# Earlier loads around attention backward: wqkv and pk/va chunks transposed into freed buffers, x over grad_out, dv without its denominator column

## The chip, the cores and the metric

The kernel runs on one core of one Trainium2 chip. The metric is the device time of one execution in microseconds. All executions quoted here were of the undisturbed (fast) kind. A run of an experiment is always timed in rounds with the kernel before on the same chip. A **ratio** is the mean time of one kernel's fast runs over that of the other's fast runs of the same rounds, so it is not quite the ratio of the medians that stand beside it.

## The reference

One transformer block, forward and backward, for x of 2048 rows and 640 columns in bf16: layer norm, linear attention with 32 heads of 20, layer norm, gated MLP of width 1728. Outputs are the block's result and the gradients of x, wqkv, wo, w1, w3, w2.

```python
phi = lambda t: jnp.where(t > 0, t + 1, jnp.exp(t)) + 1e-6
pq, pk = phi(q), phi(k)
kv = einsum("bhsd,bhse->bhde", pk, v);  z = einsum("bhsd->bhd", pk)
o  = einsum(pq, kv) / (einsum(pq, z)[..., None] + 1e-6)
h  = x + reshape(o) @ wo          # of layernorm(x)
h2 = h + (silu(n @ w1) * (n @ w3)) @ w2     # n = layernorm(h)
# then jax.vjp with grad_out
```

## The kernel before

The kernel keeps z as a 21st column of each head's kv block, so a head has DA = 21 columns where the gradient of v has DH = 20. It was tuned already: TensorE runs nearly without a gap, and all else is arranged beside it. The stretch that matters here has five stages, named after their matmuls:

1. **ghn loop** (attention backward), one step for each of 16 row tiles t: 54 matmuls for the gradient at the second norm from gg (loaded as `ggb`, 1.7 MB for two tiles), and between them `h<-woT,ghT` and three more small products of earlier tiles. SyncE loads and transposes what they need.
2. **gwo**: 160 matmuls for the gradient of wo, with the last tiles of attention backward between them.
3. **two jobs and trk**: two blocks of the gradient of wqkv (16 matmuls each, a "job"), and 12 transposes of the kv gradient.
4. **dv loop**: 16 steps that make the gradients of v (L910) and k (L731 into g_k), from pk and va loaded transposed in four chunks, with jobs between.
5. **jobs and gxn**: more jobs, then the product with wqkv transposed (`wqT`) from the transposed gradients (`gT`).

```python
    def b_gT(t):                                   # in the ghn loop, one step after b_ghn(t)
        ghT[t] = br.tile([P, DT, P], BF16, name="ghT", bufs=2)
        dmaT(out=ghT[t][:], in_=g_h[:, t, :])
    # ... (cut)
    def load_kT(c):
        pkT[c] = dx.tile([P, DT, W], BF16, name="pkT", bufs=2)
        dmaT(out=pkT[c][:], in_=pk_d[c * W:(c + 1) * W, :])
        vaT[c] = dx.tile([P, CT, W], BF16, name="vaT", bufs=2)
        dmaT(out=vaT[c][:], in_=va_d[c * W:(c + 1) * W, :])
    # ... (cut)
    for t in range(ST):                            # the dv loop
        c, i = divmod(t, TPC)
        acc = [d_acc(), d_acc()]                   # two of six PSUM banks
        for m, a, b, bank, off, first in ND:
            T.matmul(acc[bank][:, off:off + (b - a) * DA], lhsT=pkT[c][:, m, i * P:(i + 1) * P],
                     rhs=gkv_b[:, m, a * DA:b * DA], ...)
        # ... (ScalarE evicts 20 of 21 columns to g_v: cut)
        if t in (3, 4, 5, 6, 8, 9, 10, 12):
            next(jobs, None)
        gphi(vaT[c][:, :, i * P:(i + 1) * P], gkvT, pkb[c][:, i, :], g_k[:, t, :], d_acc)
        if i == 3 and c + 2 < SC:
            load_pk(c + 2)                         # plain pk rows, for VectorE
            load_kT(c + 2)
        if t == 7:
            wqT = U1.tile([P, 15, D], BF16, name="wqT", tag="D")
            dmaT(out=wqT[:], in_=A_wqkv[:, :])     # the transposed load of wqkv
```

`dma` and `dmaT` are issued by SyncE in program order; a store of a finished block is issued by ScalarE.

Of the kernel before, what the change touches and what calls it, by code (L numbers as in the profile page):

```python
# [8 lines left out]
P = 128  # L9
BF16 = mybir.dt.bfloat16  # L10
F32 = mybir.dt.float32
# [6 lines left out]
S, D, H, F = 2048, 640, 32, 1728  # L18
DH = D // H
DA = DH + 1  # L20
C, CP = H * DA, 768
ST, DT, CT = S // P, D // P, CP // P
FT, FP = 14, 1792
FL = F - 13 * P
W, SC, TPC = 512, 4, 4
HD = D // 2
NG = 27
# [35 lines left out]
def kernel(  # L63
# [19 lines left out]
    V, A, T, G, SY = nc.vector, nc.scalar, nc.tensor, nc.gpsimd, nc.sync  # L83
    dma, dmaT = SY.dma_start, SY.dma_start_transpose
# [4 lines left out]
    xS = rows(A_x.flatten_outer_dims())  # L89
# [4 lines left out]
    out2S, out3S, out4S, out5S = rows(out_2), rows(out_3), rows(out_4), rows(out_5)  # L94
# [4 lines left out]
    pk_d = dram.tile([S, D], BF16, name="pk_d")  # L99
    va_d = dram.tile([S, CP], BF16, name="va_d")  # L100
# [6 lines left out]
    def pool(name, side="left", space=None):  # L107
        kw = dict(space=space) if space is not None else dict(side=side)
        return tc.alloc_tile_pool(name=name, bufs=1, reuse_waits="tile", **kw)

    cp = pool("cp")
    U1 = pool("u1")
# [34 lines left out]
    ln1, ln2 = Stats("ln1"), Stats("ln2")  # L147
# [4 lines left out]
    ps = pool("p1p", space=PSUM)  # L152
# [143 lines left out]
    for t in range(ST):  # L296
        g, i = divmod(t, TPC)
# [8 lines left out]
        if i == 0 and g > 0:  # L306
# [3 lines left out]
               in_=v[:, :, 0:HD].rearrange("p j (h e) -> p j h e", e=DH))  # L310
# [4 lines left out]
        if i == TPC - 1:  # L315
            sl = slice(g * TPC, (g + 1) * TPC)
# [10 lines left out]
    ps = pool("pap", space=PSUM)  # L327
# [180 lines left out]
    for c in range(SC):  # L508
# [8 lines left out]
        for fc in range(FT):  # L517
# [9 lines left out]
            if c == SC - 1 and fc == 0:  # L527
                g2 = U1.tile([P, ST, D], BF16, name="g2", tag="Q")
# [18 lines left out]
    pf.release()  # L547
    ps.release()

    br = pool("br", "right")  # L550
    ps = pool("pcp", space=PSUM)
    load_hh(1)
# [24 lines left out]
    ggb = {}  # L577

    def load_gg(j):
        ggb[j] = br.tile([P, NG, 2 * P], BF16, name="ggb", bufs=2)  # L580
        dma(out=ggb[j][:], in_=gg_d[:, j * 2 * P:(j + 1) * 2 * P].rearrange("(c p) w -> p c w", p=P))

    for fc in range(FT):
        b, i = divmod(fc, 4)
        n = P if fc < FT - 1 else FL
        acc = ps.tile([P, 2, 512], F32, name="gw", bufs=4)
        for j in range(2):
            for t in range(ST):
                T.matmul(acc[:n, j, 0:HD], lhsT=hb[b][:, t, i * P:i * P + n], rhs=g2[:, t, j * HD:(j + 1) * HD],  # L589
                         start=(t == 0), stop=(t == ST - 1))  # L590
        ob = br.tile([P, D], BF16, name="gw2o", bufs=2)
# [19 lines left out]
    g_h = bl.tile([P, ST, D], BF16, name="g_h")  # L611
    g_q = bl.tile([P, ST, D], BF16, name="g_q")
    bo = pool("bo")
    o_sb = bo.tile([P, ST, D], BF16, name="o_sb")
    ps = pool("pbp", space=PSUM)
# [111 lines left out]
    def gphi(lhsT, rhs, src, out, alloc):  # L727

        acc = [alloc(), alloc()]
        for cc, a, b, bank, off, first in GP:  # L730
            T.matmul(acc[bank][:, off:off + (b - a) * DH], lhsT=lhsT[:, cc, :], rhs=rhs[:, cc, a * DH:b * DH],  # L731
                     start=first, stop=True, skip_group_check=True)
        for bank, (a, b) in enumerate(((0, SPLIT_C), (SPLIT_C, H))):
            cs = slice(a * DH, b * DH)
            V.scalar_tensor_tensor(out=out[:, cs], in0=src[:, cs], scalar=1.0, in1=acc[bank][:, 0:(b - a) * DH],
                                   op0=ALU.min, op1=ALU.mult)
# [1 line left out]
    def b_gpq(t):  # L738
        gphi(gndT[t], kvbdT, pqb[t], g_q[:, t, :], h1)

    def wo_job(m):
        acc = ps.tile([P, 2, 512], F32, name="gwo", tag="ghn", bufs=2)
        for t0, j in ((0, 0), (0, 1), (8, 0), (8, 1)):
            for t in range(t0, t0 + 8):
                T.matmul(acc[:, j, 0:HD], lhsT=o_sb[:, t, m * P:(m + 1) * P], rhs=g_h[:, t, j * HD:(j + 1) * HD],  # L745
                         start=(t == 0), stop=(t == ST - 1))
            yield
        ob = br.tile([P, D], BF16, name="gw2o", bufs=2)
        A.copy(out=ob[:].rearrange("p (j n) -> p j n", j=2), in_=acc[:, :, 0:HD])
        A.dma_start(out=out3S[:, m, :], in_=ob[:])  # L750

    def wo_jobs():
        for m in range(DT):
            yield from wo_job(m)

    b_load(0)
    b_load(1)
    wog = wo_jobs()
    for t in range(ST):
        g = b_ghn(t)  # L760

        def part():
            next(g, None)
# [24 lines left out]
        if u >= 0:  # L788
            b_gndT(u)


    xnN = {}
    b_load_q(ST - 1)

    def load_x():
        xnN[0] = U1.tile([P, ST, D], BF16, name="xnN", tag="Q")
        for i in range(SC):
            dma(out=xnN[0][:, i * TPC:(i + 1) * TPC, :], in_=xS[:, i * TPC:(i + 1) * TPC, :])

    def norm_x(a, b):  # L800
        for j in range(a, b):
            ln1.norm(xnN[0][:, j, :], xnN[0][:, j, :], j)

    def part(n=1):
        for _ in range(n):
# [2 lines left out]
    a, b, c = ST - 1, ST - 2, ST - 3  # L808
    part()
    ln_rest.pop(a)()  # L810
    load_x()
    b_gT(b)
    part()
    b_gkv(c)
    part()
    b_go(b)
    part(2)
    b_gpq(c)
    part(3)
    b_gT(a)  # L820
    part()
    b_go(a)
    b_gndT(b)
    b_gkv(b)
    part(2)
    b_gpq(b)
    norm_x(0, 8)
    part(2)
    b_gndT(a)
    b_gkv(a)  # L830
    gkv_b = kvbd
    for m, (e0, e1) in enumerate(M_H):
        bank, off = KV_SLOT[m]
        V.tensor_tensor(out=gkv_b[:, m, e0 * DA:e1 * DA], in0=gkv[:, bank, off:off + M_W[m]],
                        in1=mask[:, m, 0:M_W[m]], op=ALU.mult)
    part(2)
    b_gpq(a)
    norm_x(8, ST)
    xnN = xnN[0]
    part(20)  # L840
    br.release()


    dx = pool("dx", "right")
    pkT, vaT, pkb, gb = {}, {}, {}, {}

    def load_kT(c):
        pkT[c] = dx.tile([P, DT, W], BF16, name="pkT", bufs=2)
        dmaT(out=pkT[c][:], in_=pk_d[c * W:(c + 1) * W, :])
        vaT[c] = dx.tile([P, CT, W], BF16, name="vaT", bufs=2)  # L850
        dmaT(out=vaT[c][:], in_=va_d[c * W:(c + 1) * W, :])

    def load_pk(c):
        pkb[c] = dx.tile([P, TPC, D], BF16, name="pkb", bufs=2)
        dma(out=pkb[c][:], in_=pk_v[:, c * TPC:(c + 1) * TPC, :])

    obs = U1.tile([P, 8, 320], BF16, name="obs", tag="W6")
    cnt = [0]
    njob = 2

    def grad_job(lhs, m, rhs, n, out):

        acc = ps.tile([P, 512], F32, name="job", bufs=njob)
        for t in range(ST):
            T.matmul(acc[:, 0:n], lhsT=lhs[:, t, m * P:(m + 1) * P], rhs=rhs(t), start=(t == 0),  # L865
                     stop=(t == ST - 1))
        ob = obs[:, cnt[0] % 8, 0:n]
        cnt[0] += 1
        A.copy(out=ob, in_=acc[:, 0:n])  # L869
        A.dma_start(out=out, in_=ob)  # L870
# [4 lines left out]
    def wq_jobs(ks):  # L875
        for m in range(DT):
            for k in ks:
                for j in range(2):
                    grad_job(xnN, m, half(gqkv[k], j), HD, out2S[:, m, k * D + j * HD:k * D + (j + 1) * HD])
                    yield  # L880

    for c in range(2):
        load_pk(c)
        load_kT(c)
    ps.release()
    ps = pool("pdp", space=PSUM)
    bo.release()
    bv = pool("bv")
    g_v = bv.tile([P, ST, D], BF16, name="g_v")
    hnN = bv.tile([P, ST, D], BF16, name="hnN")  # L890
    g_k = U1.tile([P, ST, D], BF16, name="g_k", tag="S0")
    gqkv = [g_q, g_k, g_v]
    jobs = wq_jobs((0,))
    next(jobs)
    gkvT = dx.tile([P, CT, D], BF16, name="gkvT")
    for cc, dcs in BLOCKS:
        tr = ps.tile([P, len(dcs), P], BF16, name="trk", tag="job", bufs=njob)
        for i, dc in enumerate(dcs):
            T.transpose(tr[:, i, :], gkv_b[:, dc, cc * P:(cc + 1) * P], ident[:])
        V.tensor_copy(out=gkvT[:, cc, dcs[0] * P:(dcs[-1] + 1) * P].rearrange("p (i q) -> p i q", q=P), in_=tr[:])  # L900
    next(jobs)

    def d_acc():
        return ps.tile([P, 512], F32, name="dkv", bufs=6)

    for t in range(ST):
        c, i = divmod(t, TPC)
        acc = [d_acc(), d_acc()]
        for m, a, b, bank, off, first in ND:
            T.matmul(acc[bank][:, off:off + (b - a) * DA], lhsT=pkT[c][:, m, i * P:(i + 1) * P],  # L910
                     rhs=gkv_b[:, m, a * DA:b * DA], start=first, stop=True, skip_group_check=True)
        for bank, (a, b) in enumerate(((0, SPLIT_D), (SPLIT_D, H))):
            o_ = g_v[:, t, a * DH:b * DH].rearrange("p (h d) -> p h d", d=DH)
            i_ = acc[bank][:, 0:(b - a) * DA].rearrange("p (h e) -> p h e", e=DA)[:, :, 0:DH]
            A.copy(out=o_, in_=i_)
        if t in (3, 4, 5, 6, 8, 9, 10, 12):
            next(jobs, None)
        gphi(vaT[c][:, :, i * P:(i + 1) * P], gkvT, pkb[c][:, i, :], g_k[:, t, :], d_acc)
        if i == 3 and c + 2 < SC:
            load_pk(c + 2)  # L920
            load_kT(c + 2)
        if t == 7:
            wqT = U1.tile([P, 15, D], BF16, name="wqT", tag="D")
            dmaT(out=wqT[:], in_=A_wqkv[:, :])  # L924
    for _ in jobs:
        pass
    dx.release()


    ex = pool("ex", "right")  # L930
# [30 lines left out]
    ps = pool("pep", space=PSUM)  # L961
    njob = 2
# [22 lines left out]
    ps = pool("pfp", space=PSUM)  # L985
    njob = 8
# [40 lines left out]
```

## Time and profile before

| | kernel before |
|---|---|
| median, first four runs | 874.43 us (873.98 to 874.99) |
| span of the profiled execution | 873.8 us |
| TensorE busy | 851.7 us (97%) |

Columns of a timeline are start and length in us, engine, source line, operation, output and inputs, shape and count.

### The profile page before, as it was taken

The numbers are of one execution on the slowest core, as the hardware profiler recorded it, in microseconds if no ns is written. First come the engines' busy times: TensorE is split into PE (matmuls) and PEld (weight loads), VectorE is DVE, ScalarE is ACT, GpSimd is POOL, SyncE is SP. The second block draws the span as 40 slices with busy tenths as digits, with TensorE's granted clock in tenths as the row PEclk, the third lists the DMA queues.
The fourth block names the chain that finished last, engine by engine and source line by source line (L and its number), as shares of the span: only waits on it lengthen the run. The fifth ranks groups of instructions, "written<-read, shape, count | busy, mean of one in ns | idle before, by whom it ended". The sixth has DMA issues, their size and how long they took to land.

```text
span 873.8 us, 16002 instructions
## 1 busy us (share of the span) xinstructions
PE 851.7 (97%) x6263; PEld 582.2 (67%) x6263; DVE 441.0 (50%) x1134; ACT 334.6 (38%) x643; POOL 20.4 (2%) x42
## 2 busy tenths in 40 slices
PE   6999999999999999999999999999989999999998
PEld 4776555555555555777767777777757777777776
DVE  7777688888888777200146566555312434300000
ACT  4556877655655666011111111123422333322221
POOL 3100000000000000000000000000000000000000
PEclk9999999999999999999999999999989999999999
DMA  9978583364365652999477789459996588477671
GB/s 283 251 236 272 157 253 124 110 166 146 110 162 141 198 175 99 233 242 275 138 178 170 179 202 202 90 183 187 227 199 200 119 174 172 110 172 166 157 147 38
DMA packets 338027, 153.81 MB, mean 176 GB/s; under 512 B 238112, under 2 KB 336672, under 8 KB 337952
## 3 DMA queue, kind: packets, MB, share of 16 engines
q1 hardware_dynamic: 319440, 139.60, 64.9%
q10 hardware_dynamic: 18512, 13.20, 5.1%
q8 instruction: 49, 0.80, 0.4%
q14 instruction: 26, 0.21, 0.1%
HBM read 45.20 MB, written 50.02 MB: 109 GB/s over the span
## 4 chain that ended last, share of the span: by engine, by line
PE 82%; DMA 4%; SPq 2%; DVE 1%; ACT 1%; issue 0%; ACTq 0%; DVEq 0%
PE mm L413 20%; PE job L865 20%; PE ghn L643 12%; PE gxn L954 7%; PE gw L589 7%; PE o L466 7%; DMA ghT<-g_h 2%; PE h L700 2%; PE gwo L745 2%; PE at L371 2%; SPq L924 1%; DMA vaT<-va_d 1%; DMA oT<-o_t 1%; PE h L731 1%; PE nd L334 1%; SPq L948 0%
## 5 line engine op out<-in xcount | busy, mean ns | idle before, releaser
L413 PE MATMUL mm<-hnT,w 128*128 128x512 bf16 x540 | 128.1, 379 | 0.9 <-ACT hnT L408 0.9
L865 PE MATMUL job<-gb,hnN 128*128 128x288 bf16 x960 | 117.8, 286 | 0.0
L865 PEld LDWEIGHTS <-hnN 128*128 128x128 bf16 x960 | 93.9, 98 | 23.7
L643 PEld LDWEIGHTS <-ggb 128*128 128x128 bf16 x864 | 83.0, 98 | 31.1 <-issue 0.3
L413 PEld LDWEIGHTS <-w 128*128 128x128 bf16 x540 | 52.3, 98 | 61.4 <-issue 1.4
L869 ACT CAST obs<-job 128x288 bf16<-128x288 f32 (+1 forms) x90 | 36.6, 407 | 136.8 <-PE job L865 83.0
L413 PE MATMUL mm<-g2T,w2T 128*128 128x512 bf16 x280 | 69.6, 379 | 0.0
L466 PE MATMUL o<-w,hhT 128*128 128x320 bf16 x448 | 67.8, 299 | 0.0
L954 PE MATMUL gxn<-wqT,gT 128*128 128x320 bf16 x480 | 67.5, 299 | 0.0
L643 PE MATMUL ghn<-w13a,ggb 128*128 128x320 bf16 x448 | 65.6, 299 | 0.0
L643 PE MATMUL ghn<-w13b,ggb 128*128 128x320 bf16 x416 | 63.5, 299 | 0.0
L865 PEld LDWEIGHTS <-xnN 128*128 128x128 bf16 x480 | 47.7, 100 | 23.2 <-issue 3.9
L589 PE MATMUL gw<-g,hb 128*128 128x320 bf16 (+1 forms) x448 | 61.9, 299 | 0.0
L466 PEld LDWEIGHTS <-hhT 128*128 128x128 bf16 x448 | 43.8, 98 | 23.8
L224 PE MATMUL big<-wqkv,pqT 128*128 128x320 bf16 x400 | 58.5, 304 | 0.8 <-ACT pqT L220 0.8
L954 PEld LDWEIGHTS <-gT 128*128 128x128 bf16 x480 | 47.0, 98 | 18.2
L224 PEld LDWEIGHTS <-pqT 128*128 128x128 bf16 x480 | 46.6, 99 | 18.5 <-ACT pqT L220 1.0
L425 ACT CAST ghh<-mm 128x512 bf16<-128x512 f32 x56 | 33.1, 591 | 66.9 <-issue 45.4
L666 ACT ACTIVATE y<-wb,s,ln_rs 128x640 bf16<-128x640 f32 x32 | 29.5, 920 | 66.0 <-DVE wb L662 66.0
L589 PEld LDWEIGHTS <-hb 128*128 128x128 bf16 (+1 forms) x448 | 43.9, 99 | 16.3
L657 DVE SCALAR_TENSOR_TENSOR wb<-gs,xnN 128x640 f32<-128x640 bf16 x16 | 13.2, 825 | 64.8 <-ACT gs L654 64.8
L654 ACT ACTIVATE gs<-ghn 128x640 bf16<-128x640 f32 x16 | 11.2, 703 | 88.5 <-PE ghn L643 88.5
(127 smaller groups left out, 1091.3 us busy)
## 6 DMA issues: line engine op xcount, KB each, us to landing
ggb<-gg_d SPq DMA_DIRECT2D x8, 1728.0 KB, 9.5
hh_d<-hhT SPq DMA_DIRECT2D x52, 128.0 KB, 1.9
gg_d<-gate SPq DMA_DIRECT2D x52, 128.0 KB, 1.9
gg_d<-sig SPq DMA_DIRECT2D x52, 128.0 KB, 1.8
out_dram<-obs ACTq DMA_DIRECT2D x60, 72.0 KB, 2.2
va_d<-va SPq DMA_DIRECT2D x4, 768.0 KB, 6.1
out_dram<-gw2o ACTq DMA_DIRECT2D x18, 160.0 KB, 4.8
pk_d<-pkc SPq DMA_DIRECT2D x4, 640.0 KB, 4.5
```

Source lines behind the costliest of these rows:

```text
L224: T.matmul(acc, lhsT=pqT[:, c, t * P:(t + 1) * P], rhs=wqkv[:, c, n0:n0 + HD], start=(c == 0), stop=(c == DT - 1))
L371: T.matmul(at[:, 0:HD], lhsT=oT[t][:, c, :], rhs=wo[:, c, j * HD:(j + 1) * HD], start=(c == 0 and not on_pe), stop=(c == DT - 1))
L413: T.matmul(acc[:], lhsT=w[:, c, fc * P:(fc + 1) * P], rhs=rhs[:, c, :], start=(c == 0), stop=(c == DT - 1))
L425: A.copy(out=ghh[fc][:], in_=acc[:])
L466: T.matmul(o2["ps"][:, 0:HD], lhsT=hhT[c][:, fc, i * P:(i + 1) * P], rhs=w2[:, fc, j * HD:(j + 1) * HD], start=(fc == 0), stop=(fc == FT - 1))
L589: T.matmul(acc[:n, j, 0:HD], lhsT=hb[b][:, t, i * P:i * P + n], rhs=g2[:, t, j * HD:(j + 1) * HD], start=(t == 0), stop=(t == ST - 1))
L643: T.matmul(acc[:, j, 0:HD], lhsT=ggb[t // 2][:, k, lo:lo + P], rhs=rhs[:, j * HD:(j + 1) * HD], start=(k == 0), stop=(k == NG - 1))
L666: A.activation(out=y[:], in_=wb[:], func=AF.Identity, bias=s[:, 3:4], scale=st.rs[:, t:t + 1])
L700: T.matmul(go[:, 0:HD], lhsT=ghT[t][:, c, :], rhs=woT[:, c, j * HD:(j + 1) * HD], start=(c == 0), stop=(c == DT - 1))
L865: T.matmul(acc[:, 0:n], lhsT=lhs[:, t, m * P:(m + 1) * P], rhs=rhs(t), start=(t == 0), stop=(t == ST - 1))
L869: A.copy(out=ob, in_=acc[:, 0:n])
L954: T.matmul(acc[:, j, 0:HD], lhsT=gT[t][:, k, :], rhs=wqT[:, k, j * HD:(j + 1) * HD], start=(k == 0), stop=(k == 14))
```

## The change

The intent is to keep TensorE fed from the end of attention backward to gxn. The transposed chunks of pk and va go into buffers that are free earlier, so two of them stand ahead of wqkv, whose transposed load moves to the start of gwo; x is reloaded piece by piece over the part of grad_out that is used up; and dv is made without the column that is thrown away.

```diff
+    ba = pool("ba", "right")                 # gg buffers in a pool of their own
-        ggb[j] = br.tile([P, NG, 2 * P], BF16, name="ggb", bufs=2)
+        ggb[j] = ba.tile([P, NG, 2 * P], BF16, name="ggb", bufs=2)
 ... gwo: parts reordered, two that need no late g_h come before those that do
+        order[2:6] = order[4:6] + order[2:4]
 ... ghn loop, end of step t
+        if t % TPC == 1 and t > TPC:
+            load_x(t // TPC - 1)             # x piece (4 tiles) over grad_out
+        if t >= 2 * TPC - 1:
+            norm_x(t - 2 * TPC + 1)
+        if t == ST - 2:
+            load_kT(0, ba, "ggb", 2)
 ... start of gwo
+    load_kT(1, ba, "ggb", 2)
+    load_x(SC - 1)
+    wqT = U1.tile([P, 15, D], BF16, name="wqT", tag="D")
+    dmaT(out=wqT[:], in_=A_wqkv[:, :])
 ... before the dv loop
+    load_kT(2, bv, "hnN", 1)
-        tr = ps.tile([P, len(dcs), P], BF16, name="trk", tag="job", bufs=njob)
+        tr = ps.tile([P, len(dcs), P], BF16, name="trk", tag="dkv", bufs=6)
 ... dv loop: 20 of 21 columns a head, jobs at odd steps, loads
+            gv = gkv_b[:, m, a * DA:b * DA].rearrange("p (h e) -> p h e", e=DA)[:, :, 0:DH]
-        if t in (3, 4, 5, 6, 8, 9, 10, 12):
+        if t % 2:
             next(jobs, None)
+        if t == TPC - 1:
+            load_kT(3, ba, "ggb", 2)
         if i == 3 and c + 2 < SC:
             load_pk(c + 2)
-            load_kT(c + 2)
-        if t == 7:  (wqT loaded here)
 ... (stores' ring of 8 blocks becomes 10, evictions of dv contiguous: cut)
```

## The prediction

> **What bounds the kernel now.** I read the page first, then the chain of waits in order of time, then the table of waits of the TensorE, then the timelines of TensorE, SyncE and ScalarE from 565 us to 665 us, the stretch that the diff touches. From the page:
> ```profile
> PE 851.7 (97%) x6263; PEld 582.2 (67%) x6263; DVE 441.0 (50%) x1134; ACT 334.6 (38%) x643; POOL 20.4 (2%) x42
> ...
> PEclk9999999999999999999999999999989999999999
> ```
> TensorE is busy for 851.7 of 873.8 us, so no other engine bounds the kernel, and a change that leaves the matmuls alone can win at most the 22.1 us of TensorE's idle time plus what a lower clock costs. The clock row has one dip, in the thirtieth slice (633.5 to 655.4 us). The table of busy time by stretch puts the dip there:
> ```profile
> 618.00:645.00 27.00, 25.85 (x271) 20.21 (x270) 9.28 (x22) 10.70 (x28) 0.00 (x0) 1.00 1.17 249
> 645.00:659.00 14.00, 10.64 (x58) 6.55 (x57) 0.00 (x0) 1.70 (x4) 0.00 (x0) 0.76 0.86 173
> 659.00:753.00 94.00, 94.00 (x694) 67.71 (x693) 35.49 (x89) 31.25 (x59) 0.00 (x0) 1.00 0.74 163
> ```
> (Columns: length, busy us of PE, PEld, DVE, ACT, POOL, then granted clock, DMA share, GB/s.) In 645 to 659 us TensorE is idle 3.36 us and the clock is 0.76. After that stretch TensorE never waits. The timeline of TensorE shows both halves:
> ```profile
> 642.19 4.51 PE L865 MATMUL job<-g_v,xnN 128*128 128x320 bf16 x32
> 650.06 7.39 PE L865 MATMUL job<-g_k,xnN 128*128 128x320 bf16 x32 [3.36 <-ACT obs L869]
> ```
> The same 32 matmuls take 4.51 us before the idle time and 7.39 us after it. Why it waits is in the chain of waits:
> ```profile
> 631.75 10.15 SPq L924
> ...
> 646.48 2.63 DMA gT<-g_q
> 649.19 0.36 ACTq L870
> ...
> 649.59 0.43 ACT obs L869
> ...
> 650.06 9.56 PE job L865 x48
> ```
> L924 is the transposed load of wqkv. It keeps SyncE's sequencer 10.15 us, so the transposes of g_q, g_k, g_v behind it start only at 641.94. ScalarE's store of a finished gradient block (L870) then waits for one of those transposes, although it does not use its data: in the kernel before, as built, DMAs share eight completion semaphores in turn, and a store waits for the transfer that had its semaphore last. While the store waits, ScalarE cannot evict the next block, and TensorE has only two PSUM buffers for these jobs. The other waits of TensorE from 560 to 665 us are short:
> ```profile
> PE dkv L731 <- DMA vaT<-va_d: 1.1, 2, 0.7
> PE gwo L745 <- DVE g_h L667: 0.7, 1, 0.7
> PE trk L899 <- DVE gkvT L900: 0.5, 2, 0.3
> PE dkv L731 <- ACT g_v L915: 0.4, 1, 0.4
> PE trk L899 <- ACT obs L869: 0.4, 1, 0.4
> ```
>
> **What the Trainium skill says.** "TensorE: Matmul & The Clock Gate", section Part 1, says that the array falls to half clock after at least one idle window of about 3.4 us and needs about as long busy to come back. The trace agrees: 3.36 us idle, then 48 matmuls in 9.56 us where 16 take 2.17 us elsewhere, so 3 us more. "DMA: Bandwidth & Descriptors", section Issuing engines are not separate DMA queues, says that transfers from all issuers interleave on the same 16 engines. The trace agrees in that the DMA share reaches 1.17 from 618 to 645 us, with loads from SyncE and stores from ScalarE in it. "Perfetto Trace Analysis", section Optimizing Tensor Performance, says to rotate matmul groups through PSUM banks so that evictions overlap; the trk rows above show the cost of two buffers. "Advanced Engine Details and Errata", section Memory Cachelines, says SBUF reads keep full rate while neighbours share a 16-byte line. The new dv operand reads 40 of every 42 bytes, so it should cost nothing; no row of this trace has a moving operand with such gaps.
>
> **The change part by part.**
> 1. *wqkv transposed at the start of the tail.* It goes to about 580 us, as its buffer is that of w13a, read last at about 571 us. Its 10.15 us of issue then lie beside the 28 us of gwo matmuls, and it lands (12.7 us) near 593 us, 57 us before its use. The gT transposes no longer queue behind it and their first ones run during the dv loop. Saved: 3.36 us idle and 9.56 - 3 x 2.17 = 3.05 us of low clock, 6.4 us.
> 2. *pk/va chunks in the gg buffers and in the later hnN buffer.* Chunks 0 and 1 come at about 563 and 573 us, chunk 2 at about 596 us (kvbdT lay there until the last g_pq, 594.5 us), chunk 3 after the fourth step. The waits for vaT, 0.43 + 0.72 us in the timeline, go: 1.15 us.
> 3. *Order of the gwo parts.* Two parts that need no late g_h stand before those that do. The 0.69 us wait goes; ghT of tile 14 is ready at 576.2 us (copy at 575.54 plus 0.67), and TensorE now comes to it at 576.6 us.
> 4. *kvbd transposes through six banks instead of two.* In the chain they take from 602.62 to 604.75 us, 2.13 us. Five transposes without waits take 0.28 us (the h1b row), so twelve take 0.67: 1.46 us saved.
> 5. *Jobs at every odd step.* Steps 0 to 3 no longer run without a job; the 0.41 us wait for ScalarE's g_v goes. Ten jobs and all matmuls stay.
> 6. *dv without the denominator.* 36 heads' worth of columns per step fall from 756 to 720. At the 0.36 us that a step's six matmuls take in the chain this is 0.017 us, times 16 is 0.27 us. ScalarE's two evictions per step (375 ns each) are off the path.
> 7. *x reloaded in three pieces during attention backward, normalized one tile a step.* 16 normalizations at 0.366 us (2.93 us for 8) move; VectorE, at about 60% in that loop, has a gap of 1.07 us before each g_h addition. The 640 KB pieces follow odd steps, when SyncE is idle (478.8 to 480.9 us) and DMA slack is greatest. I count 0.
> 8. *What it adds.* At step 3 SyncE issues chunk 3 before the plain pk piece 2. Chunk 3 waits for the end of step 3, which I put at 611.9 us: gwo ends at 599.7, two jobs and the transposes bring the loop's start to 604.7, and two steps with one job take 2.17 + 4 x 0.35 = 3.57 us. Its issue takes 2.6 + 3.2 us (the least in the trace), so pk piece 2 starts at 617.9 us and lands some 4.6 us later, 622.5. VectorE wants it for step 8 at 619.6 us. TensorE can do dv of step 9, a job and dk of step 9 meanwhile (2.85 us) and then needs the banks that VectorE holds: about 1.3 us of waits (estimate, with two evictions at 0.44 us).
>
> Sum: 6.4 + 1.15 + 0.69 + 1.46 + 0.41 + 0.27 = 10.4 us saved, 1.3 us added: 9.1 us, and 874.05 - 9.1 = 865.0 us.
>
> **The rivals.** *A new wait in place of the old one.* If pk piece 2 lands 3 us later than I reckon, TensorE idles over 3 us, and the clock falls as at 650 us: 3 + 3 us more, 870 us or so. For it: landing times in this stretch reach 7 us for transposes. Against: the wqkv load no longer competes here. *DMA becomes the bound in attention backward.* The transfer of ghT after a gg load takes 10 us, and TensorE waited for it 0.6 and 0.3 us; x pieces ahead of the gg loads could push it back by 2 us twice: 4 us lost, 869 us. Against: a piece comes in a gap of about 2 us in issue, and of low DMA share. *The stores stay blocked.* If ScalarE's stores still share a semaphore with a transpose that is held up, part of the 6.4 us stays: 868 to 871 us. Against: the last gT before the jobs waits only for the end of the dv loop, 13 us ahead of its first use. *The gaps in the dv operand are slow.* If the 96 matmuls took twice their time, 5.6 us more: 870 us. *The waits removed were hidden anyway.* Not so for 1 to 5: they are gaps of the engine that is busy 97% and never waits later.
>
> **Range and chances.** Nearly two thirds of the gain is part 1, which I am surest of; the rest are sub-microsecond gaps. The rivals cost 3 to 6 us each and would seldom come together, while the small gains can hardly exceed their sum; so the range leans upward: 862.0 to 869.5 us. Faster by over 2% needs 856.6 us, 17.5 us less, more than all the waits named here: 0.03. Slower by over 2% needs several rivals at once on top of no gain: 0.02. Within 2%: 0.95.
>
> **What would show it.** Part 1: no idle gap of TensorE and a clock of 1.00 between the dv loop and gxn, and L924's successor issued near 580 us. Part 2: no wait for vaT. Part 3: no wait of gwo for g_h. Part 4: two job groups some 0.7 us apart. Part 6: dv rows of 140 columns not slower than the dk rows of 140 (223 ns). Part 7: no new waits of TensorE for ghT or ggb between 480 and 570 us. Part 8: VectorE's g_k waits for pkb near 620 us, and TensorE behind it. The prediction is wrong if TensorE idles over 3 us anywhere after 570 us, or if the attention backward loop (445 to 570 us) grows by over 1 us.

## More of the kernel before

The stages can be read from the timeline of TensorE of the kernel before.

I cut it to the first matmuls of each stage:

```profile
425.14 2.08 PE L643 MATMUL ghn<-w13a,ggb 128*128 128x320 bf16 x14
...
571.63 1.25 PE L745 MATMUL gwo<-g_h,o_sb 128*128 128x320 bf16 x8
...
600.25 2.34 PE L865 MATMUL job<-g_q,xnN 128*128 128x320 bf16 x16
...
606.90 0.51 PE L910 MATMUL dkv<-kvbd,pkT 128*128 128x147 bf16 x6
...
637.85 4.51 PE L865 MATMUL job<-g_k,xnN 128*128 128x320 bf16 x32
...
659.47 4.24 PE L954 MATMUL gxn<-wqT,gT 128*128 128x320 bf16 x30
```

The differences of these starts are the lengths of the stages: 146.5, 28.6, 6.65, 30.95 and 21.6 us. The same differences are taken for every kernel below.

## The result, and the profile after

The changed kernel took 873.11 us (871.19 to 874.78, 4 runs) against 874.43 us (873.98 to 874.99, 4 runs); the ratio is 0.9984, with a 95% interval of 0.9962 to 1.0006. That is the same time. The median lies outside the range of the prediction, 862.0 to 869.5 us.

The place that the prediction counted on most did what it said. The table of busy time by stretch of the changed kernel (columns as in the prediction):

```profile
618.00:645.00 27.00, 24.25 (x259) 19.25 (x258) 9.40 (x23) 10.66 (x29) 0.00 (x0) 1.00 0.69 147
645.00:659.00 14.00, 14.00 (x106) 10.09 (x104) 0.00 (x0) 2.56 (x6) 0.00 (x0) 1.00 0.98 250
```

From 645 to 659 us TensorE has no gap now and its clock is 1.00, where it had 3.36 us of idle time and 0.76. But from 618 to 645 us it was idle 1.15 us before and is idle 2.75 us now. The same cut of TensorE's timeline as before the change:

```profile
426.59 1.67 PE L644 MATMUL ghn<-w13a,ggb 128*128 128x320 bf16 x11
...
576.41 1.25 PE L751 MATMUL gwo<-g_h,o_sb 128*128 128x320 bf16 x8
...
604.18 2.34 PE L880 MATMUL job<-g_q,g 128*128 128x320 bf16 x16
...
609.20 0.51 PE L928 MATMUL dkv<-kvbd,kT 128*128 128x140 bf16 x6
...
641.32 4.51 PE L880 MATMUL job<-g_k,g 128*128 128x320 bf16 x32
...
656.52 4.24 PE L969 MATMUL gxn<-wqT,gT 128*128 128x320 bf16 x30
```

| stage | before | after | difference | predicted |
|---|---|---|---|---|
| all before the ghn loop | 425.1 | 426.6 | +1.5 | 0 |
| ghn loop | 146.5 | 149.8 | +3.3 | 0 |
| gwo | 28.6 | 27.8 | -0.85 | -0.69 |
| two jobs and trk | 6.65 | 5.02 | -1.63 | -1.46 |
| dv loop | 30.95 | 32.1 | +1.2 | -0.5 |
| jobs until gxn | 21.6 | 15.2 | -6.4 | -6.4 |
| gxn to the end | 214.3 | 214.3 | 0 | 0 |
| span | 873.8 | 870.8 | -3.0 | -9.1 |

So three of the four stages that were to win won 8.9 us, and 6.0 us were lost elsewhere. The table of waits of TensorE, changed kernel (columns: total us, times, longest), has two rows that are new or larger; those of vaT, g_h, trk and g_v that the prediction showed are gone:

```profile
PE h L701 <- DMA ghT<-g_h: 3.8, 3, 2.3
PE dkv L928 <- DVE g_k L736: 2.7, 1, 2.7
```

**The ghn loop.** Its longest wait is after the second x piece. From SyncE's timeline and TensorE's timeline of the changed kernel:

```profile
518.64 0.58 SPq L764 DMA_DIRECT2D g<-in_A_x_dram  x1
...
522.10 0.38 SPq L582 DMA_DIRECT2D ggb<-gg_d  x1
522.58 7.39 SPq L680 DMA_TRANSPOSE ghT<-g_h  x1
```
```profile
534.77 1.53 PE L701 MATMUL h<-woT,ghT 128*128 128x320 bf16 x10 [2.28 <-DMA ghT<-g_h]
```

The x piece goes out 3.5 us ahead of the 1.7 MB gg load, the transpose of g_h stands behind both, and it lands 12.1 us after its issue. In the kernel before, it landed after at most 10.2 us, which already was some tenths of a microsecond late twice. The two other waits in this row, 0.76 us at 456 us and 0.81 us at 476 us, come before the first x piece is issued (480.9 us), so x did not cause them.

**The dv loop.** From SyncE's, VectorE's and TensorE's timelines of the changed kernel:

```profile
616.58 2.65 SPq L775 DMA_TRANSPOSE kT<-pk_d  x1
619.29 4.76 SPq L776 DMA_TRANSPOSE kT<-va_d  x1
624.17 1.09 SPq L870 DMA_DIRECT2D pkb<-pk_d  x2
```
```profile
629.63 2.48 DVE L736 SCALAR_TENSOR_TENSOR g_k<-pkb,dkv 128x360 bf16<-128x360 bf16 x6 [5.05 <-DMA pkb<-pk_d]
```
```profile
630.21 0.51 PE L928 MATMUL dkv<-kvbd,kT 128*128 128x140 bf16 x6 [2.75 <-DVE g_k L736]
```

The plain pk rows for step 8 wait in SyncE's queue behind the chunk for step 12. VectorE stands still for 5.05 us and holds PSUM banks, and TensorE runs out of them.

That left three questions: whether the 1.5 us ahead of the ghn loop is part of the change (the code there is the same), whether the x pieces or chance lengthen the ghn loop, and whether the wait for pkb can simply be taken away.

### The profile page after: what moved, and what is told of

It reads as the page before. It is cut to its first block, busy times and chain, and to the rows that moved or that the text cites. A ratio compares the mean times of both kernels' runs of the same rounds, so it can differ in the third digit from the quotient of the medians.

```text
span 870.8 us, 15966 instructions
## 1 busy us (share of the span) xinstructions
PE 847.4 (97%) x6236; PEld 580.9 (67%) x6263; DVE 441.1 (51%) x1134; ACT 334.6 (38%) x643; POOL 20.5 (2%) x42
## 4 chain that ended last, share of the span: by engine, by line
PE 75%; DMA 8%; DVE 4%; ACT 1%; issue 1%; SPq 0%; POOL 0%; DVEq 0%; ACTq 0%
PE job L880 18%; PE mm L413 17%; PE ghn L644 10%; PE gxn L969 7%; PE gw L590 7%; PE o L466 7%; DMA ghT<-g_h 5%; PE gwo L751 2%; DMA out_dram<-obs 2%; PE h L701 2%; PE at L371 2%; PE dkv L928 1%; DMA pkb<-pk_d 1%; DMA oT<-o_t 1%; ACT obs L884 1%
## 5 line engine op out<-in xcount | busy, mean ns | idle before, releaser
L880 PEld LDWEIGHTS <-g 128*128 128x128 bf16 x480 | 46.5, 98 | 17.5
L413 PEld LDWEIGHTS <-w2T 128*128 128x128 bf16 x280 | 27.2, 98 | 24.4
```

The costliest lines, as they stand in the source:

```text
L413: T.matmul(acc[:], lhsT=w[:, c, fc * P:(fc + 1) * P], rhs=rhs[:, c, :], start=(c == 0), stop=(c == DT - 1))
L880: T.matmul(acc[:, 0:n], lhsT=lhs[:, t, m * P:(m + 1) * P], rhs=rhs(t), start=(t == 0), stop=(t == ST - 1))
```

## The experiments

All experiments gave right results. Those of the first four sections ran on one chip in five rounds (kernel before: median 875.11 us, 873.21 to 876.83, 11 runs), those of the last four on another chip in five rounds (kernel before: median 874.98 us, 873.09 to 876.95, 11 runs).

### The changed kernel again

No edit.

> The changed kernel once more, for its spread and for a second trace. My theory of the lost gain: the tail from the last ghn matmul to the first gxn matmul is 7.7 us shorter (87.8 to 80.1 us), the attention backward loop is 3.3 us longer because x pieces delay the ghT transposes (3.8 us of waits of TensorE for ghT against 0.9), and 1.5 us were lost before the first ghn matmul, where the code is the same. If that last 1.5 us is chance, this trace has the first ghn matmul near 425 us again and not at 426.6; the loop and the tail should repeat within 0.5 us. Time 870 to 875 us.

Measured: 872.25 us (869.34 to 874.54, 6 runs), ratio 0.9965 (0.9946 to 0.9984). TensorE's ghn loop took 149.5 us with 3.6 us of waits for ghT in four places, so that repeats. The loss ahead of the loop does not repeat: the time from the first instruction to the first matmul of the gradient of w2, which is the same code in all kernels, agrees within 0.36 us in nine traces, this one among them, and is 1.3 us longer in the first trace of the changed kernel alone. It was chance. The dv loop took 33.3 us, 1.1 us more than the first time, so the tail did not repeat within 0.5 us. The reason is a clock that fell after the wait, which it had not done in the first trace. TensorE's timeline of this run:

```profile
628.52 0.77 PE L928 MATMUL dkv<-kvbd,kT 128*128 128x140 bf16 x6 [2.62 <-DVE g_k L736]
...
630.33 3.10 PE L880 MATMUL job<-g_q,g 128*128 128x320 bf16 x16
...
634.73 2.33 PE L880 MATMUL job<-g_q,g 128*128 128x320 bf16 x16
```

The job right after the wait takes 3.10 us and the next one 2.33 us.

### The plain pk rows first

```diff
-        if t == TPC - 1:
-            load_kT(3, ba, "ggb", 2)
         if i == 3 and c + 2 < SC:
             load_pk(c + 2)
+        if t == TPC - 1:
+            load_kT(3, ba, "ggb", 2)
```

> The changed kernel with the plain pk piece issued ahead of chunk 3 of pk and va transposed at step 3. Theory: the 2.75 us wait of TensorE for VectorE's g_k near 630 us comes from the pk piece issued behind the 7.4 us of transposes; it goes, and the kernel is 2.5 to 2.8 us faster than the changed kernel (about 870.3 us). Rival: the wait moves to the transposes of chunk 3, which now start later, as a wait of the dv matmuls of step 12 for kT; then less than 1 us is won.

Measured: 868.83 us (866.49 to 870.83, 6 runs), ratio 0.9925 (0.9905 to 0.9944), so 3.4 us under the changed kernel of the same rounds (872.25 us). The dv loop takes 29.04 us instead of 32.1 and 33.3, and TensorE waits for nothing in it. SyncE's timeline shows the pk rows for step 8 issued 8.1 us after the start of that loop, where it was 15.0 us:

```profile
614.20 0.37 SPq L870 DMA_DIRECT2D pkb<-pk_d  x1
614.70 4.28 SPq L775 DMA_TRANSPOSE kT<-pk_d  x1
```

Chunk 3, issued later, was not missed at step 12, so the rival fell. The one order of two loads cost 3 to 4 us.

### All of x in the tail

```diff
-        if t % TPC == 1 and t > TPC:
-            load_x(t // TPC - 1)
-        if t >= 2 * TPC - 1:
-            norm_x(t - 2 * TPC + 1)
 ... start of gwo
-    load_x(SC - 1)
+    for i in range(SC):
+        load_x(i)
 ... (normalizations in two groups of 8, where the kernel before has them)
```

> The changed kernel with the x reload put back where it was before: four pieces in the tail, none in attention backward, normalizations in the tail too. Theory: waits for ghT fall from 3.8 to about 0.9 us and the loop from 149.8 to about 146.5 us, 3 us won, about 870 us. Rival: the loop does not change, as the waits for ghT come from VectorE's added normalizations or from chance; or the tail gives it back, because 2.5 MB of x now share the DMA engines with chunk 1 and wqkv, and the first job waits for the last normalization.

Measured: 870.69 us (868.46 to 872.23, 6 runs), ratio 0.9943 (0.9926 to 0.9959). The ghn loop took 147.5 us with 1.6 us of waits for ghT, 2 us less than with the pieces. The dv loop gave it back: 35.1 us. SyncE's timeline shows the transposed wqkv held up by the x pieces ahead of it, 16.96 us of issue instead of 11.9, and all behind it later; TensorE's timeline shows the result:

```profile
628.05 0.51 PE L925 MATMUL dkv<-kvbd,kT 128*128 128x140 bf16 x6 [4.04 <-DVE g_k L736]
...
629.35 4.01 PE L877 MATMUL job<-g_q,g 128*128 128x320 bf16 x16
```

The wait for pkb is 4.04 us now, and the job after it takes 4.01 us instead of 2.33. So both the theory and its rival held in part: x in the loop costs there, x in the tail costs in the tail, as long as the pk rows come last.

### Only the early wqkv, in the kernel before

```diff
     load_x()
+    wqT = U1.tile([P, 15, D], BF16, name="wqT", tag="D")
+    dmaT(out=wqT[:], in_=A_wqkv[:, :])
     b_gT(b)
 ... (and not at t == 7 of the dv loop)
```

> The kernel before with one part of the change: the transposed load of wqkv issued at the start of the tail, behind x. Theory: the idle 3.36 us and the low clock near 650 us go, 6.4 us won against the kernel before (about 868 us), with clock 1.00 there. Rival: chunks 0 and 1 of pk and va, which queue behind it here, come later and the dv loop's start waits for them, up to several us back; then the 6.4 us shows between dv loop and gxn but not in the time.

Measured: 871.52 us (871.09 to 872.43, 5 runs), ratio 0.9959 (0.9944 to 0.9974), 3.6 us under the kernel before. The stage of the jobs falls from 21.6 to 15.2 us, and the clock there is 1.00. So this part alone does all that was expected of it in its own stage. The time shows less for three reasons. The dv loop grew by 1.2 us, to 32.1 us, as the rival said (chunks behind wqkv, with a new wait of 0.8 us for pkT). The ghn loop, which this edit does not touch, took 147.6 us in this trace and 146.5 us in that of the kernel before. And the trace of the kernel before showed a dear execution: of the 11 runs of the kernel before in these rounds, three had a mean clock of 1.00 and took 873.2 to 874.9 us, and eight had 0.996 to 0.998 and took 874.8 to 876.8 us. Where the clock does not fall after the idle time, part 1 is worth some 3.4 us and not 6.4 us (estimate, from the stage of 18.6 us in the next trace against 15.2 us here).

### Only the x pieces, in the kernel before

```diff
+    xnN = g2
 ... ghn loop, end of step t
+        if t % TPC == 1 and t > TPC:
+            load_x(t // TPC - 1)
+        if t >= 2 * TPC - 1:
+            norm_x(t - 2 * TPC + 1)
 ... (last piece and the other normalizations in the tail, nothing else changed)
```

> The kernel before with one part of the change alone: x reloaded over grad_out in pieces during attention backward, normalized there. So far the loop from the first ghn to the first gwo matmul took 146.5, 147.5 and 147.6 us in three traces without x pieces and 149.8, 149.5 and 147.8 in three with them. Theory: the pieces cost 1 to 3 us in the loop, and this kernel is 1 to 3 us slower than the kernel before, with waits of TensorE for ghT of 2 to 4 us; the tail gains nothing but x out of the way of chunks 0 and 1. Rival: the spread is chance of the loop in every kernel, and this kernel has the time of the kernel before within 0.7 us.

Measured: 877.1 us (875.95 to 878.83, 6 runs), ratio 1.003 (1.0012 to 1.0047). This one part is a loss of 0.3%, some 2.6 us. The ghn loop took 149.1 us with 3.2 us of waits for ghT. The dv loop took 32.1 us instead of 30.95, with 2.1 us of waits for vaT where there had been 1.15 us, so not all of the loss need lie in the ghn loop; why vaT came later was not tested. The jobs again waited for ScalarE's stores, 2.71 us at once, but here the clock stayed at 1.00 and the stage took 18.6 us instead of 21.6. The timeline of TensorE of this run shows the job after the wait at full pace:

```profile
653.39 2.33 PE L869 MATMUL job<-g_k,g 128*128 128x320 bf16 x16 [2.71 <-ACT obs L873]
```

### pk rows first, and each x piece earlier in its step

```diff
             if by_dma(t - 1):
                 b_gT(t - 1)
+        if t % TPC == 1 and t > TPC:
+            load_x(t // TPC - 1)
 ... end of step t
-        if t % TPC == 1 and t > TPC:
-            load_x(t // TPC - 1)
 ... (and the order of the loads at step 3 as above)
```

> The changed kernel with the pk piece first, and each x piece issued some 4 us earlier in its step, right behind the ghT transpose of the odd step, so that it is done before the gg load of the next step starts. Theory (x pieces delay gg and with it ghT): waits for ghT fall to 0.9 to 1.9 us, as without x pieces, and the time is 1 to 2 us under that of the kernel with the pk piece first alone. Rival (chance, or the total of bytes counts and not the place): same time within 0.7 us.

Measured: 865.73 us (865.06 to 866.82, 5 runs), ratio 0.9898 (0.9882 to 0.9915). It moves the same bytes as the kernel of the next section and is 2.95 us faster than that one by the medians of the same rounds, 2.7 us by the ratios. SyncE's timeline of this run shows the new place; the first piece is out 7.4 us ahead of the gg load instead of 3.5:

```profile
473.00 1.21 SPq L680 DMA_TRANSPOSE ghT<-g_h  x1
474.27 0.57 SPq L764 DMA_DIRECT2D g<-in_A_x_dram  x1
...
481.67 0.38 SPq L582 DMA_DIRECT2D ggb<-gg_d  x1
482.15 5.79 SPq L680 DMA_TRANSPOSE ghT<-g_h  x1
```

The ghn loop took 147.5 us. The waits for ghT sum to 1.98 us, just above what was expected, and TensorE's timeline still has one behind the second piece:

```profile
531.05 1.53 PE L701 MATMUL h<-woT,ghT 128*128 128x320 bf16 x10 [1.64 <-DMA ghT<-g_h]
```

From the ghn loop to the jobs that is all that TensorE waits, apart from 0.34 us at 454 us, before the first piece. The theory holds for the first piece only: the ghT transpose behind it lands after 9.0 us here, and after 10.2 and 10.3 us in the two traces with the late piece. Behind the second piece it lands after 11.5 us, against 10.8 and 12.0 us, so there the earlier place shows no gain. The normalizations stay at the end of the step, so this run also tells the place of the loads from them: the 2.7 us are won without moving a normalization. By the median this is the fastest kernel, and about level with the last one below.

### pk rows first, a second time

No edit against the kernel with the pk rows first.

> The changed kernel with the pk piece first, a second time, so that the two others of this call are compared with it on the same chip and a second trace of its loop is there. The dv loop again at 29 to 29.5 us without a wait for VectorE's g_k; the ghn loop anywhere from 147.5 to 150 us, if the x pieces cost on average; time about 6.5 us under the kernel before, as measured (ratio 0.9925).

Measured: 868.68 us (866.45 to 870.41, 6 runs), ratio 0.9929 (0.9911 to 0.9948), as before. The dv loop took 29.03 us. The ghn loop took 150.7 us in this trace and 147.8 us in the other of the same kernel: in this one the wait behind the second x piece, 2.10 us, was followed by a low clock. TensorE's timeline, and the table of busy time by stretch with the clock in the third column from the right:

```profile
532.55 1.85 PE L701 MATMUL h<-woT,ghT 128*128 128x320 bf16 x10 [2.10 <-DMA ghT<-g_h]
```
```profile
532.50:536.00 3.50, 3.44 (x17) 2.17 (x18) 1.98 (x4) 0.00 (x0) 0.00 (x0) 0.66 0.63 180
```

### pk rows first, and all of x in the tail

The edits of "All of x in the tail" and of "The plain pk rows first" together.

> The changed kernel with the pk piece first and all of x loaded in the tail, none in attention backward. Theory: the ghn loop takes about 147 us, 1 to 2 us less than with x pieces, but the DMA engines are so full in the tail (wqkv issued in 17 us instead of 12 in the earlier run of this kind) that pk and va chunk 2 or the pk pieces come late: 1 us or more of waits in the dv loop. Sum: within 1 us of the kernel with the pk piece first alone. Rival: the dv loop stays at 29 us, and 1 to 2 us are won.

Measured: 866.05 us (865.57 to 870.64, 6 runs), ratio 0.9911 (0.989 to 0.9931). The ghn loop took 146.9 us, with one wait for ghT of 1.0 us, and the dv loop 29.03 us. The rival held for the dv loop: with the pk rows first, the tail carries all of x at no cost that the trace shows. Against x at the end of the step 2.6 us are won by the medians and 1.6 us by the ratios, as one of the six runs took 870.64 us; the intervals of the two ratios overlap (0.989 to 0.9931 and 0.9911 to 0.9948), so this gain is likely but not clear of noise. It is about level with x earlier in the step.

## Why the prediction was wrong

**Where it was right.** Part 1 (the early wqkv) took 6.4 us from its stage, with the clock at 1.00, as worked out, though wqkv was issued at 586.3 us rather than 580. That the size fits so well is in part luck: some 3 us of it are the low clock of the trace of the kernel before, which not every execution of it has. The stores of ScalarE still wait for the completion of a gT transpose by the program, but that now lands in time. Part 3 gave 0.85 us for 0.69, part 4 gave 1.63 us for 1.46. Part 2 took the waits for vaT away. Part 6: the dv matmuls of 140 columns, with gaps in their operand, have a median of 224 ns where the dense dk rows of 140 in the same trace have 222 ns, so the gaps cost next to nothing. With the pk rows first, the dv loop is 29.03 us, 1.9 us under the kernel before; the prediction had 1.15 + 0.41 + 0.27 = 1.8 us for parts 2, 5 and 6.

**The step that failed first** is part 7: "I count 0". The four traces without x pieces in the loop (kernel before, x in the tail twice, only the early wqkv) have ghn loops of 146.5, 147.5, 146.9 and 147.6 us, mean 147.1 us. The five with pieces at the end of the step have 149.8, 149.5, 147.8, 150.7 and 149.1 us, mean 149.4 us. The pieces cost 2.3 us in the mean, and the part alone made the kernel before 0.3% slower. The transposes themselves show the path: the ghT behind the first piece lands after 9.9 to 10.6 us in these five traces and after 8.5 to 8.9 us in the four without, the one behind the second piece after 10.8 to 12.1 us and after 8.9 to 10.6 us. A sign that the prediction itself had named as proof against it, a loop over 1 us longer, came true. The prediction had named this as a rival, "x pieces ahead of the gg loads could push it back by 2 us twice", and set it aside because a piece comes when SyncE does not issue and the DMA share is low. It also counted 16 normalizations into the loop, where the diff moves nine there and leaves seven in the tail. The reason that it gave looked at the moment of the issue. The question was what the next transfer with no slack is, and that was in the numbers: ghT landed up to 10.2 us after its issue and was already 0.6 and 0.3 us late without any x.

**The second term** is part 8, sized at 1.3 us. It was 2.75 us of waiting, and 3.1 us by the dv loop with and without it (32.12 against 29.04). The chain was right; its sizes were not. The issue of chunk 3 took 7.4 us rather than "the least in the trace", 5.8, and the pk rows landed 5.4 us after their issue rather than 4.6. Taking the shortest durations for a stretch full of transfers made the wait look half as long. (The prediction's own sum, 611.9 + 2.6 + 3.2, is 617.7 and not 617.9 us.) Its own rival for this ("lands 3 us later than I reckon") came nearly true: counted from the start of the dv loop, they landed at 20.3 us rather than 17.8. That the wait grew by only 1.45 us is due to its two ends: TensorE stopped at 18.3 us rather than 17.75, and went on 0.7 us after the landing rather than 1.25.

**What it did not see** is how loosely the low clock hangs on the length of a wait. It took the low clock as a consequence of idle time over 3 us only; but even in the kernel before the clock fell at 649.15 us, when the wait that ended at 650.06 us had lasted 2.45 us. In these traces TensorE ran at a low clock after waits of 2.10, 2.62, 3.36 and 4.04 us, and at full clock after 2.28, 2.71 and 2.75 us. The packed traces hold the times at which the granted clock changes, and these sort the cases. In each of the ten traces all changes lie whole steps of 3.413 us apart. Cut into these steps, TensorE was idle for 2.10, 2.12, 2.45 and 2.56 us in the step just before each of the four slow stretches, and the clock was then 0.50 for one step (two in the kernel before). In no other step, from the first rise of the clock some 11 us into the execution to the last matmul, was it idle for more than 1.95 us: the steps cut the wait of 2.75 us into 1.95 and 0.80, that of 2.28 us into 1.35 and 0.92, that of 2.71 us into 1.34 and 1.37. So what a wait of 2 to 4 us costs depended on where it fell in the steps. As their first one begins 10.3 to 12.2 us into the execution, differently in each trace, that is chance. The changed kernel had exchanged one wait of 3.4 us for two (2.28 and 2.75 us in its first trace, 1.54 and 2.62 us in its second), and a slow stretch may or may not come on top (1.1 us in the dv loop of its second trace). This explains a part of its spread at most: its six runs of the rounds cover 5.2 us, but five of them have the same mean clock, 0.998, and still cover 3.2 us. The runs of the fastest kernel, which has no wait over 1.64 us in these stages, cover 1.8 us.

**The sum.** In the first trace, 8.9 us won in three stages, 1.2 us lost in the dv loop instead of 0.5 us won, 3.3 us lost in the ghn loop, and 1.5 us of chance make 3.0 us. Undoing the two losses, in either of two ways for x, gives 865.73 and 866.05 us, 8.9 and 7.8 us under the kernel before by the ratios, where the prediction had put 865.0 us and a gain of 9.1 us. That the two orders of loads are the cause of the missing gain is therefore shown. Of the 2.7 us between the early and the late x piece most is not low clock: the four runs of the late piece with a mean clock of 1.00 have a mean of 867.9 us, still 2.1 us over the 865.8 us of the early one. Where these 2 us lie stays open: of the ghn loops of the late piece, one (147.8 us) is hardly longer than that of the early one (147.5 us), and the other (150.7 us) has a slow stretch in it.

## What to carry to other kernels

Before a transfer is moved to where a queue looks idle, look for the next transfer behind it that lands just in time; its slack, not the moment's DMA share, is what the move spends. In a queue that issues in order, put the load that is used first first, even when the other one is the bigger or was there before. A wait of TensorE of some 2 us can cost more than its length, and whether it does is chance, so compare traces with their clock before a difference of 1 to 3 us is put down to an edit.

## What the Trainium skill lacked or had wrong

- "TensorE: Matmul & The Clock Gate", Part 1, ties the fall of the clock to at least one idle window of about 3.4 us. Here stretches of low clock followed waits of 2.10 us (0.66 in the 3.5 us after it) and 2.62 us as well, while 2.28, 2.71 and 2.75 us were followed by none. The measurement decides: 2.10 us of idle time within one step of 3.413 us were enough, and 1.95 us were not.
- "DMA: Bandwidth & Descriptors", section DMA Transpose (X-bar), gives no time for which the issue of a large transpose from HBM holds the issuing sequencer; the page's only counts of this stand elsewhere, in a table on another generation of the chip, for small tiles and for SBUF to SBUF. The transpose of wqkv (1920 columns) held SyncE 10.15 us in the kernel before, 11.9 us in the changed kernel, and 15.6 to 17.0 us behind 2.5 MB of x.
- The same page's Rules for kernel authors advise to issue a DMA early and wait late. They do not say that an early transfer spends the slack of others: x pieces issued from 481 us on, which no matmul reads before 604 us, made the loop 2.3 us longer in the mean, through a transpose behind them.
